# Hash-masked attention with a mixture of adapters: loads issued four pairs ahead, signs in PSUM, the last two pairs interleaved by thirds

## The chip, the cores and the metric

The kernel runs on one core of a Trainium2 chip. The metric is the device time in microseconds, the median of three runs; lower is better. The core has five engines that follow their own queues in order: TensorE (PE, with its weight loads as PEld), VectorE (DVE), ScalarE (ACT), GpSimd (POOL) and SyncE (SP), which here only issues DMAs.

## The reference

Inputs are q, k and v of shape (4, 8, 768, 64), a projection of 64 x 6, and the weights of a router (512 x 8) and of eight rank-16 adapters.

```python
q_bits = (q @ proj > 0); k_bits = (k @ proj > 0)        # 6 bits each, one bucket of 64
mask = q_bucket[:, :, :, None] == k_bucket[:, :, None, :]
scores = where(mask, scale * q @ k.T, -1e9)
attn = softmax(scores);  attn_out = attn @ v            # rows without a partner: the mean of v
x = attn_out as (3072, 512)
logits = x @ w_gate;  take the two best of 8, softmax over them: w
out = x + sum over the two of  w * (x @ A[e]) @ B[e]
```

## The kernel before

The 32 heads are 16 pairs p; four pairs make a batch. A pair's 2 x 768 x 768 scores are worked in nine slots s of 1024 columns: `score` (L269) multiplies `aug` tiles of 71 rows (64 features and 7 rows of signs, which push a score far down where a bit differs) into PSUM, and ACT takes the exponential into `P_` (L298). In each slot `slot` (L557) writes out by hand what else is issued; each engine's queue is in that order.

Every pair p is prepared in advance. `loadqk` (L131) fetches q and k into `nat` (three buffers), `loadv` (L143) fetches v. GpSimd casts to bf16 (`natcast`, L205), SP transposes the cast by DMA into `aug` (`xbar`, L214). VectorE transposes 32 x 32 blocks (`turn32`, L163), PE multiplies with the projection (`hash`, L171), VectorE makes signs and scales them (`sign`, L183: L188 into SBUF, L191), SP stores them to DRAM and later scatters them with four DMAs into the rows of `aug` (`signs`, L195). `shift` (L221) copies the second head's features down 64 partitions on VectorE. `vcast` (L150) makes `vb` and the sum of v on GpSimd in four instructions.

In slot terms of pair p: `natcast`, `xbar` and `turn32` for p+2 in slots 0 and 1; `shift` and `signs` for p+1 in slot 1, behind the transposes on SP; the loads of q and k for p+3 in slot 1, both on GpSimd, behind the casts; `vcast` for p+1 in slot 3; `hash` for p+2 in slots 4 and 5, `sign` in slot 6. The products with v (`uni`, `pvk`) follow the exponentials, in part in the next pair. `norm` (L332) divides, `to_bf` (L345) casts on GpSimd, `turn` transposes on PE.

The router and the adapters (`moe1`, L644) of the batch before run beside the pairs: logits (`lgz`) in slots 0 to 3 of the second and third pair of a batch, `route1` and `route_exp` in slot 4, `route2` in slot 5, `zt` in slot 6, then `delta` (product, and accumulation on VectorE, L496) and `store`.

Pair 0 is prepared apart (`start`, L509; `first`, L679): PE transposes and hashes in float32, signs go straight into `aug`. Twelve matmuls on zeros come first (L527). The last pair alone is worked by thirds of 256 queries (`uni3`, `pv3`, `norm3`, `turn3`, `lasts` at L716), so that its router can begin early; `end` (L740) holds what is left.

## Time and profile before

| | us |
|---|---|
| median of three runs (lowest, highest) | 193.98 (193.34, 193.99) |
| the profiled execution's own time | 192.23 |
| its span, first to last instruction | 190.2 |
| mean granted clock of TensorE | 0.909 of full |

A profile page shows one execution. Busy time is what an engine's instructions took; a share of 1.00 of the clock is 2.4 GHz, 0.50 is 1.2. "Idle before" names what ended the wait. A table by stretch cuts the span at given times; its DMA share is the packets' time over 16 engines, so packets that overlap on an engine can make it more than 1.

### The profile page before, as it was taken

To read this page: it belongs to the slowest core of one execution; us is meant where nothing else is said; L and a number is where in the kernel's file an instruction comes from. 1 tells how busy PE (TensorE), PEld (TensorE's weight loads), DVE (VectorE), ACT (ScalarE), POOL (GpSimd) and SP (SyncE) were. 2 spreads that over 40 slices of the span, in tenths; PEclk is the share of its full clock that TensorE was granted. 3 is DMA by queue.
4 is the path that set the end of the run, shared out by engine and by line. 5 is a ranking of instruction groups with operands and counts; after the bars stand their busy time and mean duration, and the time that the engine had idled before them with its cause. 6 is when DMAs were issued, how large, how long until landed. Compare 5 with 4: busy or idle time off the path is not lost.

```text
span 190.2 us, 5242 instructions
## 1 busy us (share of the span) xinstructions
PE 164.8 (87%) x2104; PEld 105.6 (56%) x2104; DVE 129.7 (68%) x311; ACT 144.8 (76%) x162; POOL 111.6 (59%) x173
## 2 busy tenths in 40 slices
PE   7797999859999995999998799989997997996660
PEld 2333667436475853757565657565755585775310
DVE  6599376791244667469797668687887655875681
ACT  3579589857659995699999698989997998885100
POOL 2796497996954962594668696845865807020000
PEclk9999699995559999699999999999999999999555
DMA  5984799999988799957659999998599460250016
GB/s 154 352 156 103 178 247 205 222 212 233 123 190 99 148 161 155 189 158 205 144 114 229 249 187 299 243 199 224 92 221 221 128 235 8 110 225 1 0 78 253
DMA packets 54835, 33.05 MB, mean 174 GB/s; under 512 B 44572, under 2 KB 51228, under 8 KB 54812
## 3 DMA queue, kind: packets, MB, share of 16 engines
q1 hardware_dynamic: 45852, 18.70, 47.2%
q0 software_dynamic: 8384, 12.86, 29.0%
q10 hardware_dynamic: 576, 1.18, 1.7%
q8 instruction: 16, 0.26, 0.6%
q14 instruction: 7, 0.06, 0.1%
HBM read 20.06 MB, written 7.03 MB: 142 GB/s over the span
## 4 chain that ended last, share of the span: by engine, by line
POOL 35%; DMA 19%; issue 16%; PE 12%; DVE 7%; ACT 6%; SPq 1%; POOLq 0%; DVEq 0%; ACTq 0%
DMA nat<-in_k_dram 9%; POOL nb L211 8%; POOL nat L139 7%; ACT P L298 6%; POOL vs L157 5%; DMA aug<-nb 4%; POOL vb L155 4%; POOL xb L351 3%; DMA aug<-dr 3%; PE s L291 3%; PE warm L527 3%; POOL vb L160 2%; POOL vs L159 2%; DMA vn<-in_v_dram 2%; POOL wa L120 2%
## 5 line engine op out<-in xcount | busy, mean ns | idle before, releaser
L298 ACT ACTIVATE P<-s 128x1024 bf16<-128x1024 f32 x144 | 139.6, 1025 | 24.9 <-PE s L291 24.3
L291 PE MATMUL s<-aug 71*128 71x256 bf16 (+1 forms) x396 | 91.4, 336 | 11.0 <-DMA aug<-dr 7.6
L322 PEld LDWEIGHTS <-P 128*128 128x128 bf16 x1080 | 49.9, 101 | 14.7 <-issue 2.4
L322 PE MATMUL pv<-vb,P 128*128 128x65 bf16 x1080 | 52.8, 198 | 0.0
L291 PEld LDWEIGHTS <-aug 71*128 71x128 bf16 x396 | 33.3, 100 | 34.5 <-issue 12.8
L351 POOL CAST xb<-x 128x768 bf16<-128x768 f32 x15 | 12.4, 824 | 41.4 <-DVE x L342 41.4
L169 DVE STREAM_TRANSPOSE R<-nat 128x768 f32<-128x768 f32 x30 | 28.3, 962 | 4.3 <-DMA nat<-in_k_dram 3.3
L211 POOL CAST nb<-nat 128x768 bf16<-128x768 f32 x30 | 24.5, 842 | 6.7 <-DMA nat<-in_k_dram 4.0
L496 DVE SCALAR_TENSOR_TENSOR acc<-dl,rt,x 128x512 f32<-128x512 f32 x24 | 17.5, 743 | 5.1 <-PE dl L492 4.4
L179 PE MATMUL hs<-R,hst 128*32 128x192 f32 x240 | 17.0, 363 | 0.6 <-DVE xT L362 0.6
L342 DVE TENSOR_TENSOR x<-pv,ri 128x384 f32<-128x384 f32 x30 | 16.7, 557 | 1.1
L157 POOL TENSOR_TENSOR vs<-vn 128x384 f32<-128x384 f32 x16 | 15.9, 994 | 0.0
L340 DVE RECIPROCAL ri<-pv 128x6 f32<-128x6 f32 x30 | 5.7, 191 | 14.0 <-PE pv L322 13.8
L155 POOL CAST vb<-vn 128x768 bf16<-128x768 f32 x16 | 13.3, 834 | 2.6 <-DMA vn<-in_v_dram 2.6
L422 PE MATMUL lz<-wa,xT 128*128 128x136 bf16 x96 | 11.5, 240 | 0.6 <-DVE xT L411 0.6
L188 DVE TENSOR_SCALAR sg<-hs 128x192 bf16<-128x192 f32 x15 | 5.2, 345 | 9.4 <-PE hs L179 9.4
L179 PEld LDWEIGHTS hs<-R,hst 128*32 128x32 f32 x240 | 5.6, 113 | 10.7 <-issue 7.1
L191 DVE TENSOR_SCALAR s<-sg,ssc 128x192 bf16<-128x192 bf16 x15 | 11.0, 732 | 0.5
L362 DVE COPY xT<-xtp 128x768 bf16<-128x768 bf16 x15 | 8.3, 552 | 4.5 <-PE xtp L361 4.4
L310 PE MATMUL pv<-vb,eps 128*128 128x390 bf16 x30 | 10.3, 344 | 0.0
L492 PE MATMUL dl<-Bcat,zT 128*128 128x512 bf16 x24 | 10.1, 440 | 0.1
L139 POOL DMA_DIRECT2D nat<-in_q_dram x12 | 9.4, 786 | 0.0
(70 smaller groups left out, 143.4 us busy)
## 6 DMA issues: line engine op xcount, KB each, us to landing
vn<-in_v_dram SPq DMA_DIRECT2D x16, 384.0 KB
nat<-in_q_dram POOLq DMA_DIRECT2D x12, 384.0 KB, 4.4
nat<-in_k_dram POOLq DMA_DIRECT2D x12, 384.0 KB, 6.6
out_dram<-acc POOLq DMA_DIRECT2D x6, 512.0 KB, 4.3
out_dram<-acc SPq DMA_DIRECT2D x4, 512.0 KB
nat<-in_q_dram SPq DMA_DIRECT2D x3, 384.0 KB
nat<-in_k_dram SPq DMA_DIRECT2D x3, 384.0 KB
aug<-dr SPq DMA_DIRECT2D x60, 10.5 KB
```

Of the source, the lines that this page charges most:

```text
L139: eng.dma_start(out=self.nat[p][:, i], in_=s)
L155: nc.gpsimd.tensor_copy(out=vb[:, :, 0:T, 0:D], in_=vn)
L157: nc.gpsimd.tensor_add(out=s3, in0=vn[:, :, 0:3, :], in1=vn[:, :, 3:6, :])
L169: self.nc.vector.transpose(out=self.R[p][:, i, hs, :], in_=self.nat[p][:, i, hs, :])
L179: nc.tensor.matmul(out=self.hs[p][32 * j:32 * j + 32], lhsT=self.hst[:, hf].rearrange("p b i -> p (b i)"), rhs=rhs, start=(hf == 0), stop= ...
L211: self.nc.gpsimd.tensor_copy(out=self.nb[p][:, i].rearrange("p t h d -> p h t d"), in_=self.nat[p][:, i].rearrange("p h (t d) -> p h t d", ...
L291: nc.tensor.matmul(out=ps[:, o:o + w], lhsT=aug[0:71, h, 1, kt * P:(kt + 1) * P], rhs=rhs, start=True, stop=True)
L298: nc.scalar.activation(out=self.P_[p][:, s * 1024:end], in_=ps, func=ACT.Exp, scale=128.0 if p == 0 else 0.125)
L322: self.nc.tensor.matmul(out=pv[:, i, :], lhsT=self.P_[p][:, o:o + P], rhs=vb[:, h, kt, :], start=False, stop=(kt == T - 1), skip_group_che ...
L342: nc.vector.tensor_tensor(out=self.x[b][:, :, c:c + D], in0=pv[:, :, 0:D], in1=ri.unsqueeze(2).to_broadcast([P, T, D]), op=ALU.mult)
L351: self.nc.gpsimd.tensor_copy(out=xb, in_=self.x[b][:, :, hp * P:(hp + 1) * P])
L496: nc.vector.scalar_tensor_tensor(out=self.acc[b, u][:, e, :], in0=ps, scalar=rt, in1=self.x[b][:, i, :], op0=ALU.mult, op1=ALU.add)
```

## The change

- Buffers: `nat` has four, v's tiles and sums have pools of their own, `xb` three.
- From pair 1 on the loads of q (on SP) and k (on GpSimd) for p+4 are issued in slot 5; v for p+2 in slot 1.
- `sign` for p+2 moves to slot 4, and its first result stays in PSUM, beside the hash; `shift` for p+2 goes to slot 6 and `signs` for p+2 to slot 7. `hash` moves to slots 3 and 4, `vcast` to slot 5, the first products with v to slot 5.
- Pair 1 is hashed, signed and scattered one head at a time, within pair 0. Pair 2's loads are issued by GpSimd after the first casts. The eight copies into `hst` go from GpSimd to VectorE. Six warm matmuls instead of twelve; the two hashes of the first head have a tile each; two casts go from GpSimd to ACT.
- The router: logits in slots 1 to 6, `route1` in slot 6, `route_exp` and `route2` in slot 7, `zt` in slot 0 of the next pair. The mask of the two best, its product and its sum become one instruction per tile with an accumulator.
- Pairs 14 and 15 are worked together by thirds of the queries, in 18 steps (`late`); the end has a new order, and four accumulations there are split into an ACT copy with scale and a GpSimd add.

The diff's core (lines without a sign stand unchanged or around):

```diff
         self.singles = pool("singles", 1)
-        self.natp = pool("natp", 3)
+        self.natp = pool("natp", 4)
+        self.vnp = pool("vnp", 3)
...
-        self.xbp = pool("xbp", 4)
+        self.xbp = pool("xbp", 3)
...
+    def blocks(self):
+        for i in range(4):
+            for f in range(2):
+                self.nc.vector.tensor_copy(out=self.hst[32 * i:32 * i + 32, f, 0:6, i],
+                                           in_=self.proj3[32 * f:32 * f + 32, 0:6])
...
+    def hash(self, p, hf, js=range(4)):
...
+        if p not in self.hs:
+            self.hs[p] = self.ps_n.tile([self.P, 12, 32], F32, tag="n", name=f"hs{p}")
+        for j in js:
             rhs = self.R[p][:, j % 2, j // 2, :].rearrange("p (t f c) -> p f t c", f=2, c=32)[:, hf]
...
-    def sign(self, p):
+    def sign(self, p, r0=0, r1=128):
...
-        sg = self.sgp.tile([P, T, 32], BF16, tag="sg", name=f"sg{p}")
-        nc.vector.tensor_scalar(out=sg, in0=self.hs[p], scalar1=0.0, scalar2=0.5,
+        sg = self.hs[p][r0:r1, 6:12]
+        nc.vector.tensor_scalar(out=sg, in0=self.hs[p][r0:r1, 0:6], scalar1=0.0, scalar2=0.5,
                                 op0=ALU.is_gt, op1=ALU.subtract)
...
+        s2 = self.sgp.tile([P, T, 32], BF16, tag="s2", name=f"s2{p}_{r0}")
+        nc.vector.tensor_scalar(out=s2[r0:r1], in0=sg, scalar1=self.ssc[r0:r1], scalar2=None, op0=ALU.mult)
+        if p not in self.dr:
+            self.dr[p] = self.scr.tile([T, P, 32], BF16, tag="dr", name=f"dr{p}")
+        nc.sync.dma_start(out=self.dr[p].rearrange("t p c -> p t c")[r0:r1], in_=s2[r0:r1])
...
+    def signs(self, p, js=range(4)):
...
-        for j in range(4):
+        for j in js:
...
     def score(self, p, s, between=()):
         nc, S, P, T = self.nc, self.S, self.P, self.T
-        last = p == self.N - 1
+        last = p >= self.N - 2
...
+    def norm3(self, p, u, xb_eng, x=True):
...
+        pv = self.pv[p, "u", u]
+        if x != "late":
+            ri = self.rg[p, u] = self.smallp.tile([P, 2, 2], F32, tag="ri", name=f"ri{p}_{u}")
+            nc.vector.reciprocal(out=ri, in_=pv[:, :, :, D])
+            xb = self.xb[p, u] = self.xbp.tile([P, 2, P], BF16, tag="xb3", name=f"xb3_{p}_{u}")
+        ri, xb = self.rg[p, u], self.xb[p, u]
+        xv = self.x[b][:, 2 * u:2 * u + 2, hp * P:(hp + 1) * P]
+        outs = [xv] if x else []
+        if xb_eng == "dve":
+            outs.insert(0, xb)
+        for o in outs:
+            nc.vector.tensor_tensor(out=o.rearrange("p e (h d) -> p h e d", h=2), in0=pv[:, :, :, 0:D],
+                                    in1=ri.unsqueeze(3).to_broadcast([P, 2, 2, D]), op=ALU.mult)
...
+        for a, p in enumerate(ps):
+            for e in range(2):
+                nc.tensor.transpose(out=t[:, a, e, :], in_=self.xb[p, u][:, e, :], identity=self.ident_bf)
+        h = ps[0] % self.PPB
+        f = nc.scalar.copy if eng == "act" else nc.vector.tensor_copy
+        f(out=self.xT[b][:, h:h + n, 2 * u:2 * u + 2], in_=t)
...
-        nc.vector.tensor_mul(out=gw, in0=m, in1=e)
+        ss = self.smallp.tile([P, n], F32, tag=f"ss{n}", name=f"ss{b}_{I[0]}")
+        for i in range(n):
+            nc.vector.scalar_tensor_tensor(out=gw[:, i, :], in0=lz[:, i, 0:E], scalar=top[:, i, 1:2],
+                                           in1=e[:, i, :], op0=ALU.is_ge, op1=ALU.mult,
+                                           accum_out=ss[:, i:i + 1])
...
+    def dacc(self, b, i, eng=None):
+        nc = self.nc
         u, e = divmod(i, 2)
         if (b, u) not in self.acc:
-            self.acc[b, u] = self.x3.tile([P, 2, self.Dm], F32, tag="acc", name=f"acc{b}_{u}")
-        nc.vector.scalar_tensor_tensor(out=self.acc[b, u][:, e, :], in0=ps, scalar=rt,
-                                       in1=self.x[b][:, i, :], op0=ALU.mult, op1=ALU.add)
+            self.acc[b, u] = self.x3.tile([self.P, 2, self.Dm], F32, tag="acc", name=f"acc{b}_{u}")
+        dl, rt, x, acc = self.dl[b, i], self.zT[b, i][1], self.x[b][:, i, :], self.acc[b, u][:, e, :]
+        if eng == "act":
+            nc.scalar.activation(out=acc, in_=dl, func=ACT.Copy, scale=rt)
+            nc.gpsimd.tensor_add(out=acc, in0=acc, in1=x)
+        else:
+            nc.vector.scalar_tensor_tensor(out=acc, in0=dl, scalar=rt, in1=x, op0=ALU.mult, op1=ALU.add)
...
-        for i in range(12):
+        for i in range(6):
...
+        h = [self.ps_s.tile([self.P, 2, 512], F32, tag="s", name=f"h{j}") for j in range(2)]
...
-        self.hash_here(0, h)
         self.tcopy(1, "act")
-        self.hash_here(1, h)
-        self.cast(0, 0, "act")
+        self.hash_here(0, h[0])
+        self.hash_here(1, h[1])
...
         self.natcast(1, 0)
+        self.cast(0, 3, "pool")
         self.natcast(1, 1)
+        self.cast(1, 3, "pool")
         self.xbar(1, 0)
...
+        for i in range(2):
+            self.loadqk(2, i, None, nc_g)
+        self.vcast(0)
...
+    def first(self, s):
+        v = self.hb if s else None
+        if s == 0:
+            v = self.hb = [self.ps_v.tile([self.P, 512], F32, tag="v", name=f"hb{e}") for e in range(2)]
+            self.cast(0, 2, "act")
+            self.hash_here(2, v)
+            self.turn32(1, 0, 0)
+            self.turn32(1, 1, 0)
+            self.blocks()
+        if s == 1:
+            self.cast(1, 2, "act")
+            self.hash_here(3, v)
+            self.sign_here(2, 0, v[0])
+            self.sign_here(2, 1, v[1])
+        if s == 2:
+            for f in range(2):
+                self.hash(1, f, (0, 1))
+            self.sign(1, 0, 64)
+            self.sign_here(3, 0, v[0], 0, 1)
+            self.sign_here(3, 1, v[1], 0, 1)
+            self.turn32(1, 0, 1)
+            self.turn32(1, 1, 1)
+        if s == 3:
+            self.sign_here(3, 0, v[0], 1, 3)
+            self.sign_here(3, 1, v[1], 1, 3)
+            self.shift(1)
+            self.signs(1, (0, 1))
+            self.loadv(1)
+        if s == 4:
+            for f in range(2):
+                self.hash(1, f, (2, 3))
+            self.sign(1, 64, 128)
+            self.natcast(2, 0)
+            self.natcast(2, 1)
+            for i in range(2):
+                self.loadqk(3, i, None, self.nc.gpsimd)
+        if s == 6:
+            self.xbar(2, 0)
+            self.xbar(2, 1)
+            self.signs(1, (2, 3))
+            self.loadv(2)
+        if s in (5, 6):
+            self.turn32(2, s - 5)
+        if s in (7, 8):
+            self.hash(2, s - 7)
+        if s == 8:
+            self.sign(2)
...
+    def pvs(self, p, s):
+        A, B = (0, 0), (-1, 1)
+        PV = {0: [(B, 0), (B, 1)], 1: [(B, 2), (B, 3)], 2: [(B, 4), (B, 5)], 5: [(A, -1), (A, 0)],
+              6: [(A, 1), (A, 2)], 7: [(A, 3)], 8: [(A, 4), (A, 5), ((0, 1), -1)]}
...
+    def slot(self, p, s):
+        nx, n2, n3 = p + 1, p + 2, p + 3
+        self.score(p, s)
+        if p == 0:
+            self.first(s)
+        self.pvs(p, s)
+        if p == 0:
+            return
+        if s in (3, 4):
+            self.hash(n2, s - 3)
+        if s == (2 if p == 1 else 0):
             self.norm(p - 1, 0)
+        if s == (4 if p == 1 else 3):
             self.norm(p - 1, 1)
             self.to_bf(p - 1)
+        if s in (0, 1):
             self.natcast(n2, s)
             self.xbar(n2, s)
             self.turn32(n2, s)
         if p == 1 and s == 1:
             self.shift(2)
             self.signs(2)
+            self.vcast(1)
+            self.loadqk(n3, 0)
+            self.loadqk(n3, 1, None, self.nc.gpsimd)
+        if s == 1:
+            self.loadv(n2)
+        if s == 4:
+            self.sign(n2)
+        if s == 5:
+            self.vcast(nx)
+            if nx == self.N - 2:
+                self.vcast(n2)
+            self.loadqk(p + 4, 0)
+            self.loadqk(p + 4, 1, None, self.nc.gpsimd)
+        if s == 6:
+            self.shift(n2)
+        if s == 7:
+            self.signs(n2)
             self.turn(p - 1)
+        self.moe(p, s)
         if s == 6 and p >= 8 and p % 4 < 2:
             for u in ((0,), (1, 2))[p % 4]:
                 self.store(p // 4 - 2, u, None, self.nc.gpsimd)
...
+        hp = p % self.PPB
+        G = ((0, 1, 2), (3, 4, 5))
+        m = (self.ps_m, "m")
+        if b >= 0 and hp in (1, 2) and 1 <= s:
+            g = G[hp - 1]
+            c = (0, 0, 3, 6, 8, 10, 12) if hp == 2 else (0, 2, 4, 6, 8, 10, 12)
+            if s < 7:
+                for a in range(c[s - 1], c[s]):
+                    self.lgz(b, g, g[a // 4], (a % 4,), m)
             if s == 6:
+                self.route1(b, g)
+            if s == 7:
+                self.route_exp(b, g)
+                self.route2(b, g)
+        if b >= 0 and hp in (2, 3) and s == 0:
+            self.zt(b, (G[hp - 2],), m)
+        D = {3: {2: 0, 4: 1, 6: 2}, 0: {0: 3, 2: 4, 4: 5}}.get(hp, {})
         if hp == 0:
             b -= 1
...
+    def late(self, g):
+        N = self.N
+        p, q = N - 2, N - 1
+        b = self.B - 1
+        u, r = divmod(g, 6)
+        m, n = (self.ps_m, "m"), (self.ps_n, "n")
+        G0, G1 = (0, 1, 2), (3, 4, 5)
+        self.score(p + r // 3, 3 * u + r % 3)
+        if g < 3:
+            self.pvk(p - 1, 1, 2 * g)
+            self.pvk(p - 1, 1, 2 * g + 1)
+        for t in {15: (12, 13), 16: (14,), 17: (15,)}.get(g, (g - 3,)):
+            if t >= 0:
+                self.thirds(t)
+        if g == 0:
+            self.norm(p - 1, 0)
+            self.zt(b - 1, (G0,), m)
+        if g == 3:
+            self.norm(p - 1, 1)
+            self.to_bf(p - 1)
+        if 1 <= g < 7:
+            for a in (2 * g - 2, 2 * g - 1):
+                self.lgz(b - 1, G1, G1[a // 4], (a % 4,), m)
+        if g == 6:
+            self.route1(b - 1, G1)
+        if g == 7:
+            self.route_exp(b - 1, G1)
+            self.route2(b - 1, G1)
+        if g == 8:
+            self.turn(p - 1)
+        if g == 9:
+            self.zt(b - 1, (G1,), m)
+        D = {2: 0, 4: 1, 6: 2, 11: 3, 13: 4, 14: 5}
+        if g in D:
+            self.delta(b - 1, D[g], n)
+        if g in (5, 12, 15):
+            self.store(b - 1, g // 5 - 1)
+        I = ((0, 1), (2, 3))
+        if g in (10, 16):
+            self.turn3((p, q), g // 16)
+        if g in (11, 12):
+            for i in I[0]:
+                self.lgz(b, I[0], i, (0, 1) if g == 11 else (2, 3), m)
+            if g == 12:
+                self.route1(b, I[0])
+        if g == 13:
+            self.route_exp(b, I[0])
+            self.route2(b, I[0])
+        if g == 15:
+            self.zt(b, (I[0],), m)
+        if g == 17:
+            for i in I[1]:
+                self.lgz(b, I[1], i, range(4), m)
+
+    def thirds(self, t):
+        p = self.N - 2
+        w, r = divmod(t, 6)
+        if r % 3 == 0:
+            self.uni3(p + r // 3, w)
+        self.pv3(p + r // 3, w, r % 3)
+        if r % 3 == 2 and t < 17:
+            self.norm3(p + r // 3, w, "pool")
 
...
     def end(self):
         b = self.B - 1
+        q = self.N - 1
+        S, m, n, v = (self.ps_s, "s"), (self.ps_m, "m"), (self.ps_n, "n"), (self.ps_v, "v")
         I, J = (2, 3), (4, 5)
         self.route1(b, I)
+        self.thirds(16)
+        self.turn3((q - 1,), 2, v)
+        self.dmm(b, 0, n)
         self.route_exp(b, I)
+        self.dacc(b, 0, "act")
+        self.thirds(17)
         for i in J:
             self.lgz(b, J, i, range(3), S)
+        self.norm3(q, 2, "dve", False)
+        self.turn3((q,), 2, v, "act")
+        self.route2(b, I)
+        self.dmm(b, 1, n)
         for i in J:
             self.lgz(b, J, i, (3,))
         self.route1(b, J)
+        self.dacc(b, 1, "act")
+        self.zt(b, (I,), m, "act")
         self.route_exp(b, J)
+        self.store(b, 0)
         self.route2(b, J)
+        self.norm3(q, 2, None, "late")
+        self.dmm(b, 2, n)
+        self.dmm(b, 3, m)
+        self.zt(b, (J,), S)
+        self.dacc(b, 2, "act")
+        self.dacc(b, 3, "act")
+        for e in range(2):
+            self.dmm(b, 4 + e, v)
+            self.dacc(b, 4 + e)
+            self.store(b, 2, e, (self.nc.sync, self.nc.scalar)[e])
+        self.store(b, 1)
 
 @with_exitstack
 def tile_hash_attn__then__mixture_of_adapters_kernel(
```

## Rows read from the trace of the kernel before

**Rows 1.** The page's first part: busy us (share of the span) and instructions of each engine.
```profile
PE 164.8 (87%) x2104; PEld 105.6 (56%) x2104; DVE 129.7 (68%) x311; ACT 144.8 (76%) x162; POOL 111.6 (59%) x173
```

**Rows 2.** Busy time by stretch, cut at the first exponential of a pair: head, then pairs 0, 2, 3, 7, 9, 10.
```profile
core 0: us, PE busy (x) PEld busy (x) DVE busy (x) ACT busy (x) POOL busy (x), PEclk, DMA share, GB/s
0.00:10.17 10.17, 7.93 (x37) 3.56 (x39) 6.82 (x19) 4.18 (x8) 5.45 (x26) 1.00 0.78 262
10.17:21.48 11.31, 9.93 (x82) 4.53 (x82) 9.36 (x18) 8.68 (x10) 8.03 (x10) 0.89 0.61 122
...
30.89:42.42 11.53, 8.68 (x132) 5.67 (x129) 9.16 (x15) 8.65 (x10) 10.52 (x15) 1.00 1.17 205
42.42:56.63 14.21, 14.21 (x125) 8.19 (x122) 4.12 (x9) 9.11 (x9) 10.40 (x14) 0.52 1.02 174
...
87.18:95.77 8.59, 8.59 (x129) 5.51 (x126) 7.46 (x14) 8.44 (x9) 4.17 (x7) 1.00 0.76 193
...
106.39:116.21 9.82, 9.13 (x141) 6.23 (x138) 6.31 (x21) 8.86 (x10) 7.82 (x12) 1.00 1.10 226
116.21:126.26 10.05, 9.13 (x141) 6.23 (x138) 7.89 (x23) 8.86 (x10) 7.39 (x11) 1.00 1.15 239
```

**Rows 3.** Busy time by stretch, same columns: pairs 1 to 13, pairs 14 and 15, tail.
```profile
21.48:154.09 132.61, 122.12 (x1681) 80.14 (x1679) 91.43 (x204) 113.13 (x122) 93.00 (x130) 0.93 0.94 190
...
154.09:174.06 19.97, 17.64 (x271) 14.00 (x267) 13.00 (x40) 17.94 (x20) 4.70 (x7) 1.00 0.29 112
174.06:190.20 16.14, 7.17 (x47) 3.36 (x46) 9.14 (x34) 0.84 (x4) 0.40 (x1) 0.56 0.24 97
```

**Rows 4.** ACT's timeline: start, us, instruction, and in brackets the idle time before it.
```profile
21.48 1.02 ACT L298 ACTIVATE P<-s 128x1024 bf16<-128x1024 f32 x1 [1.92 <-PE s L291]
...
42.42 1.94 ACT L298 ACTIVATE P<-s 128x1024 bf16<-128x1024 f32 x2 [2.36 <-PE s L291]
...
152.10 6.86 ACT L298 ACTIVATE P<-s 128x1024 bf16<-128x1024 f32 x7 [0.42 <-PE s L291]
```

**Rows 5.** The chain of waits in order of time: start, us, what.
```profile
65.96 10.31 DMA nat<-in_k_dram
...
97.58 6.05 DMA aug<-nb
```

**Rows 6.** Timelines of VectorE and of GpSimd (POOL) in the first 32 us.
```profile
8.06 2.23 DVE L264 TENSOR_SCALAR aug<-h 6x384 bf16<-6x384 f32 x6 [0.60 <-PE h L258]
...
22.45 0.83 POOL L155 CAST vb<-vn 128x768 bf16<-128x768 f32 x1 [2.58 <-DMA vn<-in_v_dram]
...
25.26 0.82 POOL L211 CAST nb<-nat 128x768 bf16<-128x768 f32 x1
```

**Rows 7.** Groups of instructions by line: count, busy us, mean ns, and idle time before them.
```profile
L157 POOL TENSOR_TENSOR vs<-vn 128x384 f32<-128x384 f32 x16 | 15.9, 994 | 0.0
...
L250 ACT ACTIVATE aug<-qkT 64x384 bf16<-64x384 f32 x3 | 1.5, 517 | 0.0
```

**Rows 8.** The instructions of line 457: duration ns min/median/max, first and last start.
```profile
L457 DVE TENSOR_TENSOR gw<-m,e x9: 164/680/719, 70.1 to 181.5; 128x24 f32<-128x24 f32 x6, 128x16 f32<-128x16 f32 x3
```

**Rows 9.** The timeline of pair 13, GpSimd and VectorE, near 149.5 us.
```profile
149.50 0.99 POOL L157 TENSOR_TENSOR vs<-vn 128x384 f32<-128x384 f32 x1
...
149.82 0.71 DVE L457 TENSOR_TENSOR gw<-m,e 128x24 f32<-128x24 f32 x1 [0.98 <-ACT e L447]
```

**Rows 10.** The timeline of the tail.
```profile
173.04 1.02 ACT L298 ACTIVATE P<-s 128x1024 bf16<-128x1024 f32 x1
...
175.22 0.28 PE L410 MATMUL xt<-ident_bf,xb 128*128 128x128 bf16 x2 [1.05 <-POOL xb L401]
...
175.59 1.03 PE L422 MATMUL lz<-wa,xT 128*128 128x136 bf16 x8
...
177.77 0.41 ACT L399 CAST xb<-x 128x256 bf16<-128x256 f32 x1 [0.41 <-DVE x L395]
...
182.99 3.38 DVE L496 SCALAR_TENSOR_TENSOR acc<-dl,rt,x 128x512 f32<-128x512 f32 x5
```

299 lines of the change are left out of this document (58 added, 241 removed), and 3 rows, old and new, of the table PV.

## The prediction

> **What bounds the kernel now.** I read the busy shares first [rows 1]: PE 164.8 us and ACT 144.8 of a span of 190.2, so no engine is full and the question is where the time is lost. Then the span cut at the first exponential of each pair [rows 2]. Pair 7 takes 8.59 us with PE and ACT both busy nearly throughout: that is a pair in which nothing waits, 8.59 / 9 = 0.954 per step. Pair 3 takes 14.21 with PE busy all the time and a granted clock of 0.52, that is, mostly the 1.2 GHz level; pairs 9 and 10 take 9.82 and 10.05. The wider stretches [rows 3] give pairs 1 to 13 as 132.61, where 13 pairs like pair 7 would take 111.7. About 21 us there are waits. The rest is the head (10.17), pair 0 (11.31), the last two pairs (19.97) and the tail (16.14).
>
> ACT's timeline shows where [rows 4]: the long gaps stand before a pair's first exponential (1.92 and 2.36 here, two more near 2, four of 0.5 to 1.3). A shorter one of 0.42, before the eighth step, comes in the five pairs with a router (5, 6, 9, 10, 13). Pair 3 follows the 2.36 gap: PE went idle, the clock fell, and the pair cost 5.6 more than pair 7. The chain of waits names what is late [rows 5]: a k load that took 10.31 from issue to landing, a transpose 6.05. The order explains it. `loadqk(p+3)` stands at slot 1 of pair p, its cast and transpose at the start of pair p+1, and on SP the scatter for pair p+2 stands behind that transpose: a late load delays SP, and so a pair's start.
>
> **The change, part by part**, against the profiled execution's span.
>
> *Head, 10.17 now.* The first signs wait 0.60 for the k hash because both hashes share one tile [rows 6]; separate tiles end that. Six warm matmuls fewer free PE earlier, but VectorE, which takes the first copy, is still in its memsets then, so I count nothing for them. The eight `hst` copies leave GpSimd for VectorE, behind the first score: hidden while the hash of pair 1 is late anyway. Pair 2's loads move from SP to GpSimd, two issues behind four casts; the first use is half a pair later. I take 0.95 off: 9.2. Bounds: 1.6 off, or nothing where the clock rises later (a rival).
>
> *Pair 0, 11.31 now, with the 1.92 gap.* Two casts move from GpSimd onto ACT, 2 x 0.517 [rows 7]. Nine steps give 8.6, with the casts 9.6, and 0.2 for ramps. The gap was the scatter of pair 1 (issued at slot 4); head 0's half now goes at slot 3 and only that half is needed at the start. So 9.85.
>
> *Pairs 1 to 13, 132.61 now.* Loads go from 8 slots ahead of their cast to 13: some 12.4 us at 0.954 against the 10.31 seen worst. Scatters go from slot 1 of the pair before to slot 7 of the one before that, 11 slots ahead against 8, and no longer behind the next transposes. GpSimd loses one issue in two, SP gains it; SP's load stands between the sign store and the scatter and waits for nothing, as there are now four buffers. That should empty the gaps at pair starts, and with them the fall in pair 3. The router is spread to slot 6, its exponential to slot 7, and the transpose `zt` to slot 0 of the next pair, still two slots behind its exponential. What ACT's gap hangs on is the small product `gw`, 164 to 719 ns [rows 8]; it becomes three instructions per group with one operand in PSUM. Bounds: 3 x 0.164 = 0.5, or 3 x 0.719 = 2.2; I take 0.5, since the 0.164 rows are those with GpSimd idle. The row shows that spread; the Trainium skill (SBUF — State Buffer, Who interferes with whom) says that a VectorE instruction with two SBUF inputs contends with GpSimd's reads and one with a single SBUF input does not. By that rule the new form never waits, and the gap would go wholly, 0.2 us a router pair under my sum; the trace agrees where I looked: a `gw` of 0.71 beside a GpSimd add that ends with it [rows 9].
> So 8 pairs at 8.6 and 5 at 9.0 are 113.8. Against that: pair 1 starts 2.4 us earlier than now, while pair 3's loads go out later, from GpSimd behind two casts; pair 1's `vcast` (2.8 us on GpSimd, from its first row to the next cast [rows 6]) stands behind them, and `uni(1)` at slot 5 waits for it. From these I estimate 1.5 us lost there. And 2.5 for transfers that are still late in pairs 2 to 4, where the weight loads fall, and 8 to 10, where the stores do. Together 117.8. Signs held in PSUM only shorten VectorE's queue; VectorE has 91.43 busy of 132.61 [rows 3], so I cost them at nothing; should VectorE fill up, their gain would be on the path.
>
> *Pairs 14 and 15, 19.97 now.* 18 steps of 0.954 are 17.2, ACT's bound; no hash, no loads, the router work spread out. I add 0.7 for three router hand-overs: 17.9.
>
> *Tail, 16.14 now.* From the last exponential's end (174.06) the last accumulations run until 186.37 and the stores to 190.2: 12.31 and 3.83 [rows 10]. Of the 12.31 go: 1.16 in which PE waits for the second third's cast (to 175.22), 1.03 of logits of tiles 2 and 3, both now within the steps; four of the five accumulations in a row, 4 x 0.676; and ACT's cast, 0.41, since VectorE writes the bf16 form itself. That leaves 7.0, and with the stores, and 0.2 for hand-overs, 11.0. Four accumulations become an ACT copy and a GpSimd add; the nearest row, 0.994 for 384 columns [rows 7], gives 1.3 for 512, so four in a row are 5.3, the first about 1 behind the exponential: hidden, by little. Bounds of this part: 10 and 13.
>
> Sum: 9.2 + 9.85 + 117.8 + 17.9 + 11.0 = 165.75, and 2.03 outside the span as now: 167.8 against 192.23. That execution lies 0.9% under the median of 193.98; in the same ratio the median becomes 169.3.
>
> **The rivals.**
> *The DMA engines become the bound.* Their share was 0.94 over pairs 1 to 13, 124.7 us of packet time; in 117.8 that is 1.06. For it: pairs 9 and 10, at 1.10 and 1.15, were no faster than 9.94 on average. Against: pair 2 reached 1.17 [rows 2], and shares count packets that overlap. Price: 13 x 9.94 = 129.2, 11.4 more, 180.8 as a median. On the split of q and k over SP and GpSimd, the Trainium skill (DMA: Bandwidth & Descriptors, Issuing engines are not separate DMA queues) says that it saves issue time only, as all share 16 engines. By that rule the earlier issue brings reach, not bandwidth, and this rival is what it gives if bandwidth lacks.
> *The clock rises late.* Now the head's row has 1.00 [rows 2], after 12 dense warm matmuls; with 6 TensorE may stay at 1.2 GHz through pair 0, which then costs what pair 3 did, 14.21 for 9.85, and the head gains nothing: 5.3 more, 174.7.
> *The change doesn't do what it says:* the waits at pair starts stay, for instance because GpSimd, blocked at `to_bf`, now issues k loads as late as before. Pairs 1 to 13 keep 132.6, the rest gains: 14.8 more, 184.3. Against: GpSimd is busy 4.17 of pair 7's 8.59 [rows 2], so it comes to slot 5 in time.
> *Slower: VectorE held at `shift`.* It now stands at slot 6 of the pair whose slots 0 and 1 issue its transposes. With 6.05 to landing [rows 5] and 1.3 for the issue they land at 7.4, and slot 6 comes at 5.7: VectorE waits 1.7, with `xT`, the router and the next norm behind it. Where that grows by a further 2, PE idles, the clock falls, and a pair costs 5.6 more plus the 2.4 wait. Three such pairs eat the gain, four make 32 more, 201.6.
>
> **How the numbers follow.** My forecast has 0.62, the DMA bound 0.17, the late clock 0.10, the unmoved waits 0.06, the held VectorE 0.05. The forecast's own bounds: 6.1 less with nothing lost in pair 1 or to transfers, the router gap gone and the best head, 163; up to 175 with the tail at 13 and 4 us more of waits. The range reaches over the first two rivals to 181. Half a per cent is what a measurement of this kernel can tell from no change. All cases but the held VectorE are faster: 0.94; slower 0.05; 0.01 between.
>
> **What would show it.** Right: ACT's gaps before first exponentials under 0.3 from pair 2 on, no stretch at half clock between head and tail, pairs 1 to 13 near 118, last exponential to end near 11, first exponential near 9.2. Wrong: pairs near 9.9 with the DMA share over 1.1 (first rival); pair 0 at a clock near 0.5; VectorE's longest waits on the transposes at `shift`, with PE idle behind them; a tail whose last accumulation waits for GpSimd.

## The result, and the profile after

The changed kernel has a median of 189.19 us in four runs (187.21 to 194.63) beside 193.66 for the kernel before on the same chip; the ratio is 0.968, interval [0.964, 0.973]. It is faster, as forecast, but by 3% where 13% were forecast: 169.3 was wrong by 20 us, and the time lies above the range. Executions of one and the same kernel differ here by several per cent (the kernel before ran from 187.75 to 200.15 on one chip), so ratios and intervals leave disturbed runs out, down to two in some cases, and medians over all runs stand beside them.

The first part of the page of the changed kernel, from an execution that took 194.63 of its own, answers to [rows 1]: PE and ACT are a little busier than before, though the point of the change was to have fewer waits.

```profile
PE 169.4 (88%) x2112; PEld 109.6 (57%) x2114; DVE 124.1 (64%) x340; ACT 148.9 (77%) x169; POOL 110.1 (57%) x162
```

Where the time is shows in the busy time by stretch of that execution, cut as in [rows 2, 3] at first exponentials: head, pairs 0, 1 and 2, pairs 3 to 13, then pairs 7, 9 and 10 out of these, pairs 14 and 15, tail.

```profile
core 0: us, PE busy (x) PEld busy (x) DVE busy (x) ACT busy (x) POOL busy (x), PEclk, DMA share, GB/s
0.00:8.98 8.98, 7.14 (x31) 3.23 (x33) 6.72 (x19) 4.27 (x8) 2.64 (x17) 1.00 0.67 219
8.98:25.10 16.12, 12.56 (x82) 4.86 (x82) 12.86 (x30) 9.81 (x11) 11.37 (x15) 0.84 0.78 164
25.10:39.26 14.16, 10.49 (x151) 7.18 (x149) 4.19 (x10) 8.78 (x9) 8.37 (x12) 0.86 0.95 161
39.26:52.54 13.28, 13.28 (x128) 7.71 (x126) 8.04 (x13) 9.22 (x10) 9.84 (x13) 0.57 0.95 197
52.54:159.91 107.37, 101.73 (x1414) 66.75 (x1410) 73.32 (x193) 95.21 (x105) 67.34 (x93) 0.95 0.74 179
87.65:96.89 9.24, 9.15 (x132) 5.93 (x129) 8.72 (x19) 8.80 (x10) 5.23 (x8) 1.00 0.80 204
105.59:117.48 11.89, 8.95 (x141) 6.11 (x137) 5.52 (x21) 8.65 (x11) 8.78 (x13) 1.00 0.82 220
117.48:131.38 13.90, 13.41 (x132) 8.25 (x133) 7.01 (x27) 9.15 (x11) 5.74 (x8) 0.63 0.74 224
159.91:181.82 21.91, 20.85 (x296) 18.28 (x298) 13.85 (x55) 18.08 (x21) 5.55 (x11) 0.84 0.31 122
181.82:192.90 11.08, 3.37 (x33) 1.57 (x30) 5.12 (x27) 3.56 (x9) 5.01 (x4) 0.74 0.37 146
```

Head and tail came as forecast. Pair 0 takes 16.12 instead of the 11.31 of before, pairs 1 and 2 together 27.44 against 20.94, and pair 2 runs at 0.57, most of it at 1.2 GHz. From pair 3 on most pairs take 8.3 to 9.4, but pair 9 takes 11.89 and pair 10, after it, 13.90 at a clock of 0.63; the last two pairs, 21.91 at 0.84, have such a stretch too. Before, one pair ran mostly at the lower clock [rows 2].

The engines' waits of the same execution (engine, line, tile, releaser: us in all, times, longest) name two that are new or have grown, first VectorE's at `shift` and then SyncE's before the scatter in `signs`:

```profile
DVE aug L230 <- DMA aug<-nb: 25.9, 11, 6.7
...
SPq L207 <- DMA dr<-s: 49.9, 16, 5.3
```

In the kernel before the second of them was small (same view, its own lines):

```profile
SPq L202 <- DMA dr<-s: 5.2, 5, 2.6
```

SyncE's timeline, then VectorE's and ACT's, over pairs 8 and 9 of the changed kernel show how one becomes the other:

```profile
102.91 0.42 SPq L198 DMA_DIRECT2D dr<-s  x1
103.42 0.49 SPq L143 DMA_DIRECT2D nat<-in_q_dram  x1
108.38 1.42 SPq L207 DMA_DIRECT2D aug<-dr  x4
109.89 2.56 SPq L222 DMA_TRANSPOSE aug<-nb  x2
...
115.33 0.64 DVE L230 COPY aug<-aug 64x1536 bf16<-64x1536 bf16 x1 [4.68 <-DMA aug<-nb]
...
116.45 0.22 ACT L452 ACTIVATE e<-d 128x24 f32<-128x24 f32 x1 [3.14 <-DVE d L443]
```

The sign store of pair 10 is issued at 102.91. SyncE then takes one load of q and stands until 108.38, for the store to land. Pair 9 has begun at 105.59; the transposes of its slots 0 and 1 were ready behind GpSimd's casts (from 105.90, 1.59) and go out at 109.89 only. They land at 115.25, `shift` in slot 6 has held VectorE for 4.68, the router behind it is late, ACT stands 3.14 before the ninth step, and TensorE, idle meanwhile, runs the next pair at a clock of 0.63.

### The profile page after: what moved, and what is told of

It is laid out like the page before. It is cut to its first block, busy times and chain, and to the rows that moved or that the text cites. A ratio compares the mean times of both kernels' runs of the same rounds, so it can differ in the third digit from the quotient of the medians.

```text
span 192.9 us, 5338 instructions
## 1 busy us (share of the span) xinstructions
PE 169.4 (88%) x2112; PEld 109.6 (57%) x2114; DVE 124.1 (64%) x340; ACT 148.9 (77%) x169; POOL 110.1 (57%) x162
## 4 chain that ended last, share of the span: by engine, by line
PE 31%; ACT 17%; DMA 16%; DVE 12%; POOL 11%; issue 7%; SPq 2%; POOLq 1%; DVEq 0%
ACT P L303 16%; PE s L296 14%; DMA dr<-s 10%; PE pv L327 4%; DMA aug<-nb 4%; POOL nb L216 3%; PE hs L183 3%; PE lz L430 2%; DMA aug<-dr 2%; DVE aug L269 2%; DVE zm L469 2%; POOL xb L356 2%; DVE gw L464 2%; POOL vs L161 2%; PE ztp L487 1%
## 5 line engine op out<-in xcount | busy, mean ns | idle before, releaser
L296 PE MATMUL s<-aug 71*128 71x256 bf16 (+1 forms) x408 | 95.2, 343 | 6.1 <-DMA aug<-dr 3.7
L296 PEld LDWEIGHTS <-aug 71*128 71x128 bf16 x408 | 36.7, 103 | 25.5 <-issue 10.6
L327 PE MATMUL pv<-vb,P 128*128 128x65 bf16 x1008 | 50.8, 201 | 0.0
L230 DVE COPY aug<-aug 64x1536 bf16<-64x1536 bf16 x15 | 13.5, 897 | 26.9 <-DMA aug<-nb 25.9
L173 DVE STREAM_TRANSPOSE R<-nat 128x768 f32<-128x768 f32 (+1 forms) x32 | 28.4, 908 | 0.1
L183 PE MATMUL hs<-R,hst 128*32 128x192 f32 x240 | 20.0, 374 | 2.1 <-DVE R L173 1.2
L512 DVE SCALAR_TENSOR_TENSOR acc<-dl,rt,x 128x512 f32<-128x512 f32 x20 | 14.6, 735 | 6.2 <-PE s L296 3.7
L192 DVE TENSOR_SCALAR hs<-hs 128x192 f32<-128x192 f32 (+1 forms) x16 | 5.9, 366 | 18.1 <-PE hs L183 18.0
L347 DVE TENSOR_TENSOR x<-pv,ri 128x384 f32<-128x384 f32 x28 | 15.6, 557 | 1.0
L143 POOL DMA_DIRECT2D nat<-in_k_dram x14 | 10.3, 733 | 0.0
L430 PEld LDWEIGHTS <-xT 128*128 128x128 bf16 x96 | 6.5, 103 | 4.5 <-issue 3.6
```

Source lines behind the costliest of these rows:

```text
L173: self.nc.vector.transpose(out=self.R[p][:, i, hs, :], in_=self.nat[p][:, i, hs, :])
L183: nc.tensor.matmul(out=self.hs[p][32 * j:32 * j + 32, 0:6], lhsT=self.hst[:, hf].rearrange("p b i -> p (b i)"), rhs=rhs, start=(hf == 0), ...
L230: self.nc.vector.tensor_copy(out=aug[0:64, 1], in_=aug[64:128, 0])
L296: nc.tensor.matmul(out=ps[:, o:o + w], lhsT=aug[0:71, h, 1, kt * P:(kt + 1) * P], rhs=rhs, start=True, stop=True)
L327: self.nc.tensor.matmul(out=pv[:, i, :], lhsT=self.P_[p][:, o:o + P], rhs=vb[:, h, kt, :], start=False, stop=(kt == T - 1), skip_group_che ...
L347: nc.vector.tensor_tensor(out=self.x[b][:, :, c:c + D], in0=pv[:, :, 0:D], in1=ri.unsqueeze(2).to_broadcast([P, T, D]), op=ALU.mult)
```

## The experiments

**Theory A**: SyncE's wait in `signs` (slot 7) makes the next transposes late, and `shift` (slot 6) hands this on to VectorE. **Theory B**: the eight `hst` copies on VectorE (`blocks`) delay pair 0 and all up to pair 2. Against both stood a delay by the loads themselves.

**r_after**: the changed kernel again, unedited.

> The changed kernel itself once more, for a profile of one of its more frequent executions. Theory A (SyncE, waiting in signs for the landing of the sign store, issues the next pair's transposes late; VectorE stands at shift for them; the router, zt and PE behind it; the clock falls): 0.965 to 0.970 of before, with VectorE's gap before shift over 3 us in pairs 9 and 13 and an exponential gap of 2 to 3 us at their last step, even where the clock does not fall afterwards. Theory B (only a fallen clock in pairs 2, 10 and 14 makes the loss, from another cause): those gaps are absent in this execution.

Ratio 0.982 [0.972, 0.992], median 189.05; 0.965 to 0.970 was expected. Its profile has a span of 188.8: head 9.23, pair 0 15.96, pairs 1 and 2 27.60, pairs 3 to 13 106.10, pairs 14 and 15 18.85, tail 11.01. By stretch, pairs 3 to 13 and pair 11, then VectorE and GpSimd late in pair 10:

```profile
52.79:158.89 106.10, 102.88 (x1411) 67.19 (x1408) 77.10 (x193) 95.16 (x104) 67.90 (x93) 0.94 0.76 181
126.30:141.51 15.21, 14.73 (x123) 8.39 (x124) 8.54 (x20) 9.20 (x10) 5.74 (x8) 0.55 0.43 114
...
122.35 2.45 DVE L230 COPY aug<-aug 64x1536 bf16<-64x1536 bf16 x1 [1.98 <-DMA aug<-nb]
122.77 1.60 POOL L216 CAST nb<-nat 128x768 bf16<-128x768 f32 x2
```

Now pair 10 stalls, by 2.24 before its ninth step, pair 11 takes 15.21 at 0.55, and pairs 9 and 13, which theory A had named, are clean: the place changes, the kind doesn't. But the wait is only half of this stall. VectorE waited 1.98 at `shift`, and then the copy itself, beside GpSimd's next casts, took 2.45, where the shortest take 0.56.

**e_signs_next**: the scatters of pairs 3 to 14 behind the next pair's transposes.

```diff
         if s == 1:
             self.loadv(n2)
+            if p > 1:
+                self.signs(nx)
...
         if s == 7:
-            self.signs(n2)
+            if p == self.N - 3:
+                self.signs(n2)
```

> signs of pairs 3 to 14 back in slot 1 of the next pair, behind the transposes on SyncE. Theory A: transposes are issued within 2.5 us of a pair's start, VectorE's gap before shift falls under 0.5 us, the gaps at the last step of pairs 9 and 13 go, pairs 10 and 14 keep the full clock: 0.93 to 0.95 of before. Rival (transposes are late because their casts on GpSimd are, behind the stores): gaps in pairs 9 and 13 stay, 0.96 to 0.97. Rival (a scatter in slot 1 is too late for the pair's start): gaps of 1 us or more before the first exponentials come back, 0.96 or more.

Ratio 0.950 [0.933, 0.967], median 185.84. The table by stretch of this kernel for pairs 3 to 13:

```profile
51.25:150.19 98.94, 97.06 (x1411) 64.33 (x1408) 76.01 (x193) 94.64 (x104) 68.52 (x94) 1.00 0.85 194
```

And SyncE's timeline in pairs 8 and 9, to be held against the one above, with its wait before the scatters in the whole execution:

```profile
101.94 0.38 SPq L198 DMA_DIRECT2D dr<-s  x1
102.42 0.49 SPq L143 DMA_DIRECT2D nat<-in_q_dram  x1
106.49 2.65 SPq L222 DMA_TRANSPOSE aug<-nb  x2
...
109.86 0.31 SPq L207 DMA_DIRECT2D aug<-dr  x1
...
SPq L207 <- DMA dr<-s: 7.4, 4, 2.8
```

98.94 instead of 106.10, a clock of 1.00 throughout, and no gap before a ninth step over 0.15. The transposes of pair 9 (from 105.33) go out 1.2 into it, where they went 4.3 into it above, and the scatter, 7.9 after its store, finds it landed: SyncE's wait there is 7.4 us in all, against 36.1 in r_after and 49.9 in the first profile. Theory A holds here. What stays: pair 0 at 16.10, pair 2 cold (0.54, most of it at 1.2 GHz), waits of 1.1 to 1.7 at `shift` in pairs 4, 9 and 10, where under 0.5 was expected, and a gap of 1.26 at the start of pair 5, since the scatter now goes out later.

**e_shift_s8**: the other way to keep VectorE free, `shift` and `signs` both two slots and one slot later.

```diff
-        if s == 6:
-            self.shift(n2)
         if s == 7:
-            self.signs(n2)
             self.turn(p - 1)
         self.moe(p, s)
+        if s == 8:
+            self.shift(n2)
+            self.signs(n2)
```

> shift and signs moved to slot 8, behind the router's instructions on VectorE; SyncE still waits in signs. Theory A says that the link is VectorE standing at shift with the router behind it: transposes stay late, but the gaps at the last step of pairs 9 and 13 go, and with them the half clock after them: 0.93 to 0.95 of before. If the loss came through late scatters or late loads, nothing changes: 0.965 to 0.97.

Ratio 1.016 [0.995, 1.037]: no gain, where theory A expected 0.93 to 0.95. VectorE's, SyncE's and ACT's timelines at the start of pair 8 (95.64) show why:

```profile
94.77 2.42 DVE L230 COPY aug<-aug 64x1536 bf16<-64x1536 bf16 x1
...
97.21 1.37 SPq L207 DMA_DIRECT2D aug<-dr  x4
98.67 2.55 SPq L222 DMA_TRANSPOSE aug<-nb  x2
...
100.30 2.16 ACT L303 ACTIVATE P<-s 128x1024 bf16<-128x1024 f32 x2 [1.76 <-PE s L296]
```

The scatter writes rows of `aug` that `shift` reads, so it goes right behind `shift`, at 97.21, and the transposes behind it go out 3.0 into the pair. With `shift` late, SyncE's queue is late in every pair, `norm` and `turn32` stand behind `shift`, and the stall moves to the fourth or fifth step: 1.4 to 1.9 in pairs 3, 4, 5, 8 and 12 and 2.66 in the last two pairs; pair 12 takes 15.38 and the last two 24.47. The ninth steps are clean, as expected, but with the transposes still late on SyncE the stall only changes its place.

Its pairs 1 and 2 took 19.63, against 27.60 in r_after, though pair 0 was as long (16.01). Up to pair 2's scatter SyncE's order is the same in both; here the two scatters went out 5.9 and 4.4 after their stores, there 7.6 and 4.9, and pair 2 kept the full clock. So what pairs 1 and 2 lose hangs also on how fast these transfers land; whether the edit has a part in that no run shows.

**e_hst_pool**: the eight copies back on GpSimd, in the constants; `blocks` isn't called.

```diff
+        for i in range(4):
+            for f in range(2):
+                nc.gpsimd.tensor_copy(out=self.hst[32 * i:32 * i + 32, f, 0:6, i],
+                                      in_=self.proj3[32 * f:32 * f + 32, 0:6])
...
-            self.blocks()
```

> The eight copies into hst back on GpSimd before the first casts, 2.4 us off VectorE in pair 0. Theory A for the first pairs (VectorE is the bound of pair 0, 16.1 us): pair 0 shorter by 1 to 2.5 us, 0.955 to 0.965 of before. Rival (pair 0 and 1 are held by late landings of the sign store and of pair 3's loads): pair 0 shorter, but pair 2 starts no earlier, 0.965 to 0.97.

Ratio 0.941 [0.928, 0.955]. VectorE's timeline in pair 0 of the changed kernel has the copies ahead of the signs of the third quarter, which the fourth step needs:

```profile
10.10 2.36 DVE L114 COPY hst<-proj 32x6 f32<-32x6 f32 x8
12.48 1.03 DVE L269 TENSOR_SCALAR aug<-hb 6x384 bf16<-6x384 f32 x2
```

Without them those signs start at 11.15, and the table by stretch of e_hst_pool gives pairs 0, 1 and 2:

```profile
9.09:23.01 13.92, 11.87 (x82) 4.67 (x82) 9.43 (x21) 9.80 (x12) 10.23 (x14) 0.90 0.60 164
23.01:32.89 9.88, 9.61 (x154) 6.72 (x152) 7.65 (x11) 8.77 (x9) 8.05 (x11) 0.97 0.99 202
32.89:42.53 9.64, 8.88 (x126) 5.53 (x123) 4.34 (x9) 8.46 (x10) 8.64 (x13) 1.00 1.08 178
```

Pair 0 is 2.0 shorter, and pair 2 starts 6.4 earlier than in r_after (32.89 against 39.29). But pair 3 then stands 3.44 before its fifth step and takes 15.6, and pairs 3 to 13 stay at 107.94: the knot on SyncE is still there. B holds for pair 0; how long pairs 1 and 2 are hangs on both.

**e_both**: the two edits together.

> The scatters of pairs 3 to 14 go back to slot 1 of the next pair, behind the transposes, and the eight copies into hst go back to GpSimd; all else is the changed kernel. Theory A (SyncE, standing in signs for the landing of a sign store, issues the next transposes late) and theory B (the eight copies lengthen VectorE's queue in pair 0 and so everything up to pair 2's start) act in different stretches, so their gains should add: pair 0 near 14 us, pair 1 near 10, pairs 3 to 13 near 99 in all, ratio to the kernel before 0.89 to 0.92, about 173 to 177 us. If instead the two only trade one startup delay (the loads of pairs 2 to 4 are what is late, and starting pair 2 earlier merely moves the wait to pair 3), the ratio stays at 0.93 to 0.95 and pair 3 or 4 begins with a gap over 2 us and runs at 1.2 GHz.

Ratio 0.930 [0.920, 0.940], median 183.06, where 0.89 to 0.92 was expected. Pair 0 is 14.14, pairs 1 and 2 22.53, pairs 3 to 13 101.49: less than the two gains in sum, since pair 3 starts with a gap of 2.09, as the rival has it, though at the full clock, and pair 10 has 2.16 before its ninth step. That last one is VectorE at `shift` again, standing 3.35, but for transposes that were behind no scatter this time (SyncE, then VectorE):

```profile
109.07 4.34 SPq L226 DMA_TRANSPOSE aug<-nb  x2
117.72 1.00 DVE L234 COPY aug<-aug 64x1536 bf16<-64x1536 bf16 x1 [3.35 <-DMA aug<-nb]
```

The first went out 0.1 before the pair's start (109.18) and the second 1.6 into it; they landed 8.6 after the first. Here the landing itself is late, and theory A isn't the cause.

**e_both_load2**: e_both with pair 2's loads back on SyncE, in `start`.

```diff
+        self.loadqk(2, 0)
+        self.loadqk(2, 1)
...
-        for i in range(2):
-            self.loadqk(2, i, None, nc_g)
```

> As e_both, with the loads of pair 2 issued by SyncE in start, as in the kernel before, rather than by GpSimd after the first casts. If late loads of pair 2 hold the transposes of pairs 2 and 3, pair 2 or 3 starts 1 to 2 us earlier than in e_both and the ratio falls by 0.005 to 0.01; if the loads only compete with pair 0's own, the head grows by 0.3 to 1 us and nothing is won; if neither, the two are within 0.5% of each other.

Ratio 0.931 [0.922, 0.940], median 186.64: no difference in the ratios, though the medians lie 3.6 us apart. In its profile pair 1 starts at 21.72 and pair 2 waits 6.44, behind a sign store that took 5.31 to land and a scatter that took 6.05. And the old stall is back, with the scatter out of the way: pair 10 stands 2.25 before its ninth step, and pair 11 runs cold (pairs 3 to 13, pair 11, then VectorE in pair 10).

```profile
52.66:159.42 106.76, 102.80 (x1411) 66.81 (x1408) 77.52 (x193) 95.06 (x104) 68.58 (x94) 0.94 0.80 179
126.94:142.04 15.10, 14.62 (x123) 8.29 (x124) 8.54 (x20) 9.21 (x11) 5.74 (x8) 0.56 0.69 150
...
123.23 2.20 DVE L234 COPY aug<-aug 64x1536 bf16<-64x1536 bf16 x1 [2.24 <-DMA aug<-nb]
```

**e_both_drfirst** and **r_drfirst**, the same kernel twice: e_both with the scatter of pair 1's second half behind pair 2's sign store.

```diff
         if s == 6:
             self.xbar(2, 0)
             self.xbar(2, 1)
-            self.signs(1, (2, 3))
...
         if s == 8:
             self.sign(2)
+            self.signs(1, (2, 3))
```

> As e_both, with the scatter of pair 1's second half moved from slot 6 to slot 8 of pair 0, behind pair 2's sign store on SyncE. Theory A says that pair 2's sign store stands in SyncE's queue behind the wait for pair 1's second sign store: without it the store is issued about 2 us earlier and pair 2 starts 1 to 2 us earlier; pair 1's scatter goes out one or two us later, and pair 1's second half is needed only from its fourth step on, so pair 1 does not suffer by more than 0.5 us. Rival: the scatter waits for the landing of the store in either place and pair 1 stalls at its fourth or fifth step by 1 to 3 us, ratio 0.005 to 0.015 higher than e_both.

> The fastest variant so far run again (scatters of pairs 3 to 14 in slot 1 of the next pair, the eight copies into hst on GpSimd, the scatter of pair 1's second half in slot 8 of pair 0), to give it an interval. Theory A expects a ratio to the kernel before of 0.90 to 0.93, with pairs 3 to 13 between 98 and 102 us in all; a ratio over 0.94 would say that the 174.7 and 177.1 us of its best runs were luck of the transfers.

The store of pair 2 goes out at 22.81 instead of 26.35, as theory A has it, but pair 1 waits 2.48 before its fifth step where e_both had 1.40, as the rival has it, and runs cold; pairs 1 and 2 take 22.74 against 22.53, so nothing is won there. Median 180.93 the first time; the second time 179.49 beside 193.46, ratio 0.951 with a wide interval [0.913, 0.990]. Over 0.94 was to mean that the 174.74 and 177.08 of the first time were luck of the transfers. Pairs 3 to 13 of the second, by stretch:

```profile
46.46:145.64 99.18, 97.03 (x1411) 64.23 (x1408) 75.14 (x193) 94.71 (x105) 71.15 (x98) 1.00 0.86 199
```

**e_shift1**: r_drfirst with `shift` of pairs 3 to 14 also back in slot 1 of the next pair.

```diff
             if p > 1:
+                self.shift(nx)
                 self.signs(nx)
...
-        if s == 6:
+        if s == 6 and p == self.N - 3:
             self.shift(n2)
```

> As the run before, with shift of pairs 3 to 14 moved from slot 6 back to slot 1 of the next pair, ahead of the scatter. Theory C: what is left of the stalls before the ninth step in router pairs (2.29 us in pair 10 of one run) is VectorE standing at shift for transposes that landed 8.6 us after the first of them was issued, so it needs no scatter in front of it; then no pair from 3 to 13 has a gap over 1 us at its ninth step, VectorE's waits on aug<-nb fall to under 1 us each, and the ratio is 0.005 to 0.02 lower. Rival: shift in slot 1 stands ahead of norm and turn32 and holds them for the same landing, gaps of about 1 us move to pair starts, and the ratio is the same or up to 0.01 higher.

Ratio 0.965 [0.952, 0.979], so not lower. Theory C is right in its mechanism: VectorE's waits at `shift`, 5.5 us in r_drfirst, fall to one of 0.4, and no ninth step waits over 0.15.

```profile
DVE aug L234 <- DMA aug<-nb: 0.4, 1, 0.4
```

But pair 4 starts with a gap of 1.53 and runs cold, and pair 11 with one of 3.41. The chain of waits of e_shift1 before it:

```profile
113.89 1.61 POOL nb L220 x2
...
116.24 2.37 SPq L226
...
119.57 0.38 SPq L211
...
120.00 5.42 DMA aug<-dr
```

The second transpose is issued at 116.24 and takes SyncE 2.37, the scatter behind it goes out at 119.57, 5.2 into pair 10, and its landing takes 5.42. A scatter behind the transposes spares VectorE, but is late for its own pair when it lands this slowly.

**e_p0**: e_shift1 with both hashes of pair 2 in slot 8 of pair 0, and with `shift` and the load of v for pair 1 behind `sign` of its second half. Here the signs of pair 1's first head overwrite rows of its second head before `shift` copies them; the amount of work is the same.

```diff
-        if s in (7, 8):
-            self.hash(2, s - 7)
         if s == 8:
+            self.hash(2, 0)
+            self.hash(2, 1)
             self.sign(2)
...
         if s == 3:
-            self.shift(1)
             self.signs(1, (0, 1))
-            self.loadv(1)
         if s == 4:
             self.sign(1, 64, 128)
+            self.shift(1)
+            self.loadv(1)
```

> As e_shift1, with two edits in pair 0: both hashes of pair 2 go into slot 8 (now one in slot 7), and shift of pair 1 and the load of v for pair 1 go behind the sign of pair 1's second half (now ahead). Theory D: pair 0 loses 1.2 to 1.5 us before its ninth step because TensorE stands at the hash of pair 2 in slot 7 for blocks that VectorE transposes late, and pair 1 loses 1.4 to 2.5 before its fifth step because the second sign store goes out 0.8 us late behind shift; so pair 0 falls from 14.2 to about 13 and pair 1's gap by 0.8, ratio 0.01 lower than e_shift1. Rival: the score before it needs the same time, since ScalarE and TensorE in pair 0 are held by TensorE's clock, and nothing changes.

Ratio 0.948 [0.930, 0.966]. The gap before pair 0's ninth step is gone (1.49 in e_shift1), and that half of D holds. The other half failed: `shift` now waits 2.74 for the scatter, VectorE's transposes of pair 2 stand behind it, TensorE waits 2.20 for these at pair 2's hash, and pair 1's first score stands behind that hash (timelines of VectorE, and of ACT at pair 1's first exponential).

```profile
19.02 0.68 DVE L234 COPY aug<-aug 64x1536 bf16<-64x1536 bf16 x1 [2.74 <-DMA aug<-dr]
...
25.04 1.94 ACT L307 ACTIVATE P<-s 128x1024 bf16<-128x1024 f32 x2 [5.28 <-PE s L300]
```

**e_best** and **r_after_b**, on one chip: r_drfirst with the two hashes in slot 8 alone (the first hunk above), beside the changed kernel unedited.

> As r_drfirst (scatters of pairs 3 to 14 in slot 1 of the next pair, the copies into hst on GpSimd, the scatter of pair 1's second half in slot 8), with one edit: both hashes of pair 2 in slot 8 of pair 0, behind that slot's score, instead of one in slot 7. Theory D: the gap of 1.1 to 1.5 us before the ninth step of pair 0 goes, pair 0's nine steps end 1.2 us earlier, and since TensorE then works on the hash behind them, the time to pair 1's first step falls by less, 0.3 to 1 us; ratio of the medians to the kernel before about 0.92, and to the changed kernel beside it about 0.95. Rival: the gap moves whole to the start of pair 1 and nothing is won.

> The changed kernel unedited, on the same chip as the run before it, so that the two stand beside each other. Theory A expects, in whichever pairs it stalls, a wait at shift or at a pair's start of over 2 us in one to three pairs from 3 on, each with a stretch at 1.2 GHz behind it, pairs 3 to 13 at 104 to 110 us, and a ratio of 0.96 to 0.98; a run without any such stall, with pairs 3 to 13 under 101, would say that the stalls are not the rule.

Medians 182.47 and 186.73, beside 197.62 for the kernel before; ratios 0.952 [0.935, 0.969] and 0.988 [0.974, 1.001]. Pair 0 is 13.46 and its gap before the ninth step gone; r_drfirst has 13.98, but the six profiles with the copies on GpSimd and a hash in slot 7 lie between 13.09 and 14.40, so a gain of 0.5 isn't shown. Pair 1 waits 4.82 before its fifth step: TensorE stands 1.84 at the hash of pair 3, for blocks that VectorE transposes when their k load has landed, and 1.86 for the scatter of pair 1's second half, which now goes behind both hashes, at 25.32 (24.16 in e_both_drfirst). Pair 10 has the stall of e_both again, 2.24, and pairs 3 to 13 take 103.59. In r_after_b pair 2 starts with a gap of 4.98 and runs cold, pair 5 waits 2.01 before its ninth step and pair 13 1.89 before its fifth; pairs 3 to 13 take 102.48, under the 104 expected: this time no pair from 3 on fell to the lower clock. So e_best lies under both kernels by intervals that don't meet, and e_both and e_both_load2 lay under the kernel before on their chip, where the changed kernel didn't run; which variant is best these runs don't separate.

## Why the prediction was wrong

The forecast's sum inside the span was 165.75; the profile of r_after has 188.8. These 23 us are 20 in the medians, since that execution (190.52) lies 1.3 over the median of 189.19, and the forecast's median (169.3) 1.5 over its execution (167.8). Step by step:

- *Head* 9.2: measured 8.98 and 9.23. *Tail* 11.0: 11.03 (the row above reaches 0.05 past the last instruction) and 11.01. Right.
- *Pairs 14 and 15* 17.9: 18.85 where nothing stalls, 0.95 too low. The bound was taken from ACT, but TensorE is the busier one there (PE 18.41, ACT 17.87, in r_after).

```profile
158.89:177.74 18.85, 18.41 (x306) 16.26 (x303) 13.71 (x55) 17.87 (x21) 5.06 (x11) 1.00 0.36 142
```

- *Pair 0* 9.85: 15.96, 6.1 too low. The step that failed is the one that cost the copies at nothing, "hidden while the hash of pair 1 is late anyway". Their cover was looked for at the hash; in VectorE's queue they stood ahead of the signs that the next scores need. Taking them out gave 2.0. Of the rest, 3.6 against the forecast in e_best (13.46), ACT's gaps are 1.15 before the sixth step and 2.36 at pair 1's start. TensorE mostly works in both, on the second half of pair 1's hash (1.30) and on pair 2's (1.70, at the lower clock), which stand ahead of the next score, while the sum took the nine steps as those of a pair in which nothing waits. No run moved these hashes out of pair 0.
- *Pairs 1 and 2*: 27.6 against 17.2 and the 1.5 set aside, 8.9 too low. The 1.5 was an estimate for late loads; late were sign stores, whose landing SyncE waits out before each scatter, and the sum had no term for that. The chain of waits of the changed kernel up to pair 2:

```profile
19.02 7.64 DMA dr<-s
...
27.83 5.12 DMA dr<-s
...
33.37 4.71 DMA aug<-dr
```

  Two stores and a scatter one after the other, all through SyncE, and the second store could only be issued once the wait for the first was over. How much they cost varies: e_shift_s8, with the same start-up, took 19.63.
- *Pairs 3 to 13*: 11 pairs at 8.6 and 9.0 plus 2.5 for late transfers are 99.1. The changed kernel has 107.4, 106.1 and 102.5 in three profiles. With the scatter behind the transposes and `shift` in slot 6, six have 98.9, 99.1, 99.2, 101.5, 103.6 and 106.8. So the sum is what a clean execution takes, in part by luck: the 2.5 was for late transfers, but in e_signs_next pairs 6 and 7 took 9.39 and 9.24 with no gap on ACT over 0.35. What failed is the sentence that scatters go out "no longer behind the next transposes": now the transposes stood behind the scatter. The prediction asked whether the load between store and scatter waits for anything, not what the scatter itself waits for, which is the landing of the store issued 1.0 us before it. The queue's order was read for what it frees and not for what it blocks. It is the cause in the pairs where SyncE stood; in pair 10 the stall came back in three of the six profiles without it (e_both, e_both_load2, e_best).

  What all these stalls share is `shift`. In the ten profiles that have it in slot 6, a router pair's ninth step starts late by VectorE's wait at `shift` plus what the copy takes over 0.56, less 1.62, or not at all where that is negative; this holds to 0.03 us in 49 of 50 pairs, and the other ran at the lower clock. So VectorE has 1.6 us to spare there, and late issue, slow landing and a slow copy all draw on it.
- *Router*: three `gw` a group at 0.22 each with 0.08 for the accumulator, 0.5 in all as taken. The gap before the eighth step is gone in undisturbed pairs; at the ninth it is 0.15 or less in r_after and e_signs_next.

Of the **rivals**, the bound by DMA engines is false: at a share of 0.86 pairs 3 to 13 took 99.18 us. So is the late clock: TensorE was at 1.00 in the head, and fell only at about 20 us (16 in e_signs_next), after its waits in pair 0. The unmoved waits are false from pair 3 on, where r_after has no gap over 0.35 at a pair's start up to pair 13. The held VectorE, given 0.05, is what happened, at the place, by the sign (VectorE's longest waits are those at `shift`) and with the next-pair clock that it named; but it put the delay on the transposes' own landing, which came in pair 10 once the scatter was out of the way, missed that SyncE would issue them late, and asked for three or four such pairs. There were one or two in an execution of the changed kernel, 1.8 to 3.1 us each and 3 to 6.5 more in the next pair where the clock fell, so they ate a part of the gain and not all.

In all, the start-up up to pair 3 makes 15.0 of the 23 us missing, the stalls after it 7.0, the late pairs 1.0.

## What to carry to other kernels

When an instruction moves on a queue, list what it waits for at its new place and what stands behind it, also on an engine that only issues DMAs: a wait for a landing is a wait of every later issue. A chain store, landing, scatter wants its scatter behind the next urgent issue, not right behind the store, as far as its own use leaves time. And copies moved to another engine are hidden only if nothing urgent follows them there before the work that is thought to hide them ends. An engine that stands at one instruction holds all behind it: count what it has to spare there (here 1.6 us) before its inputs are let come close.
